# The last load of the experts' weights issued as 16 transfers of eight partitions in place of one of 128

## The chip, the cores and the metric

The kernel runs on one core of a Trainium2 chip. The metric is the time of one execution on the device in microseconds (us), as the median of several runs. All views of the profile come from one execution, and their times are counted from the start of its span.

## The reference, cut to what matters

Three blocks follow each other in float32. The second, a soft mixture of experts, is the one whose weights the change loads.

```python
# 1: attention packed through 32 slots per head (8 batches, 8 heads, 576 positions, 64 wide)
out = sm_attn(q, sm_attn(p, k, v), sm_attn(p, k, v))      # softmax attention, twice
x = out as rows: (4608, 512)

# 2: soft mixture of 8 experts, 4 slots each
logits = x @ phi                                          # (4608, 32)
slot_input = softmax(logits over rows).T @ x              # (32, 512)
for e in range(8):
    h = maximum(slot_input[e] @ w1[e], 0)                 # w1[e]: 512 x 1024
    slot_out[e] = h @ w2[e]                               # w2[e]: 1024 x 512
x = softmax(logits over slots) @ slot_out                 # (4608, 512)

# 3: dense layer with SoLU and layer norm
h = x @ w_in                                              # 512 -> 1024
solu = h * softmax(h)
y = (solu - mean) / sqrt(var + 1e-6) * g_ln
return y @ w_out                                          # (4608, 512)
```

Part 3 needs the outputs of all experts before its first row: each row of `x` is a mix over all 32 slots.

## The kernel before, in words

The kernel has three stages. Stage 1 is the attention, with the logits and the slot inputs summed on the way. Stage 2 sends the slot inputs through the experts and, at its end, multiplies the slot outputs into `w_in`: `sw` = `slot_out @ w_in`, which stage 3 uses in place of `w_in`. Stage 3 walks over 36 tiles of 128 rows: a product `h` with `sw` (L1416), softmax and norm statistics on DVE, ACT and POOL, two transposes, and the product `o` with `w_out` (L1592, L1598, the last tile also L1605).

All loads go out from SP, in one order fixed in the list `order`, into a ring of 14 slots of 128 x 2304 floats (four more slots join later): keys, queries, values, `w_in`, `w_out`, and then the experts' weights as 29 loads `("w", 0)` to `("w", 28)`. Those weights are cut into 256 granules of 128 x 256 floats, nine to a load. Load 27 goes out in three parts of one, four and four granules (`CUTS`), and load 28, the last, has the four granules that are left: 128 partitions of 4 KB. The function `load` (L308) issues them; the line of the experts' weights is L321.

The first four experts are computed one after the other (`mk_w1`, L1039, and `mk_w2`, L1090). The second products of the last four experts come as the last 64 granules, ordered by quarter `k` of the model width and by expert within it (`mk_block`, L1132). A block takes four granules, eight matmuls. The last two blocks are quarter 3 of experts 6 and 7: the first of them reads the last part of load 27, the second reads load 28 and nothing else reads that load. After the last block of a quarter ACT copies the sum out (L1143), PE turns it (L1147), ACT writes it to `SO`, and PE multiplies that into `sw` (L1350): quarters 0 to 2 as they come, quarter 3 at the end. Then ACT and DVE write `sw` out in two parts (L1358, L1362), and the first `h` of stage 3 follows.

The order of instructions on each engine is written out by a planner (`Plan`) before anything runs: it simulates the engines with the costs given to `op`, and the instructions are then emitted in that order. Every engine takes its instructions in that order at run time. A load stands in the plan as one step of the engine "DMA", with 317 ns a granule; the function that the step calls may issue several transfers. Semaphores are put in by the framework. A DMA from SP gets one of eight semaphores in turn, and SP does not issue it before the transfer that had the same semaphore eight issues earlier has landed.

Of the kernel before, what the change touches and what calls it, by code (L numbers as in the profile page):

```python
# [185 lines left out]
def pack_attention__soft_moe__solu_kernel(  # L186
# [13 lines left out]
    nc = tc.nc  # L200
# [20 lines left out]
    NSPLIT = 1  # L221
    CH = (0, 2, 4, 8)
    NMOVE = 4
    NRUN = 400
    NLATE = 500
    NTRY = 3500
# [26 lines left out]
    with ExitStack() as p12, tc.manual_schedule():  # L253
# [54 lines left out]
        def load(key, part):  # L308
            def go():
                if part == 0:  # L310
                    pool = W["ring2"] if key in RING2 else ring
                    loaded[key] = pool.tile([128, RW], FP32, tag="r", name="r")
                t = loaded[key]
                if key[0] in "kq":
                    c0, c1 = (1152 * c for c in halves(key)[part:part + 2])
                    nc.sync.dma_start(out=t[:, c0:c1], in_=(kT if key[0] == "k" else qT)[key[1]][:, c0:c1])
                elif key[0] == "v":
                    nc.sync.dma_start(out=t, in_=v[key[1], key[2]])
                elif key[0] == "w":
                    c0, c1 = (256 * c for c in cuts(key[1])[part:part + 2])  # L320
                    nc.sync.dma_start(out=t[:, c0:c1], in_=w12[key[1]][:, c0:c1])  # L321
                else:
                    src = (w_out if key[0] == "wo" else w_in)[key[1]].bitcast(UINT32)
                    nc.sync.dma_start(out=t[:, :2048].bitcast(UINT32), in_=src)

            return go

        def halves(key):
            return (0, 1, 2) if key[1] == 0 else (0, 2)

        def cuts(i):
            return CUTS.get(i, (0, min(9, 32 * NE - 9 * i)))
# [1043 lines left out]
        plan.goals = [(x, 1.0), (o_SIT, 0.3), (o_lo, 0.1)]  # L1376
        plan.trials = NRUN
        plan.then = [(NLATE, set(range(o_2, len(plan.ops))))]
# [7 lines left out]
    with ExitStack() as p3, tc.manual_schedule():  # L1386
# [329 lines left out]
        for k in range(NT):  # L1716
            mk_tile(k, ([*range(8), *range(32, 36), *range(8, 32)])[k])
            if k == NMOVE - 1:
                plan.moved = set(range(n0, len(plan.ops)))
# [63 lines left out]
```

## Time and profile before

| | us |
|---|---|
| median of 3 runs | 399.81 (398.6 to 400.46) |
| the profiled execution | 398.32 |
| its span in the profile | 396.5 |
| PE busy / DVE / ACT / POOL | 375.6 / 285.4 / 232.6 / 205.9 |
| stage 1 to about | 126 |
| stage 2 to about | 181 |

The profile gives, for each engine, the time in which it ran an instruction. A chain of waits is followed back from the last instruction of the kernel, at each step to what released it, so what stands in the chain is what set the end in this execution. "SPq" is SP's queue, on which DMAs are issued; "DMA" in the chain is a transfer from its issue to its landing. "PEld" is the load of a matmul's weights, which runs ahead of the matmul. [...] In the views of PE an fp32 matmul counts as two.

### The profile page before, as it was taken

To read this page: it belongs to the slowest core of one execution; us is meant where nothing else is said; L and a number is where in the kernel's file an instruction comes from. 1 tells how busy PE (TensorE), PEld (TensorE's weight loads), DVE (VectorE), ACT (ScalarE), POOL (GpSimd) and SP (SyncE) were. 2 spreads that over 40 slices of the span, in tenths; PEclk is the share of its full clock that TensorE was granted. 3 is DMA by queue.
4 is the path that set the end of the run, shared out by engine and by line. 5 is a ranking of instruction groups with operands and counts; after the bars stand their busy time and mean duration, and the time that the engine had idled before them with its cause. 6 is when DMAs were issued, how large, how long until landed. Compare 5 with 4: busy or idle time off the path is not lost.

```text
span 396.5 us, 9563 instructions
## 1 busy us (share of the span) xinstructions
PE 375.6 (95%) x3760; PEld 198.0 (50%) x3760; DVE 285.4 (72%) x563; ACT 232.6 (59%) x437; POOL 205.9 (52%) x314
## 2 busy tenths in 40 slices
PE   8888999988989999798999999999999999999996
PEld 3456566656535664553444444444444444444445
DVE  2168899997977889917997766776677667766721
ACT  1447787887644654116978665666566656665610
POOL 1032456263234556892769665556555655565540
PEclk9999999998999999999999999999999999999999
DMA  8999999999999999940367956685776766756761
GB/s 308 423 419 416 418 419 415 419 418 414 421 416 421 421 414 422 416 189 1 62 128 157 185 122 145 136 158 120 147 157 135 122 145 156 138 119 145 140 152 54
DMA packets 89420, 99.25 MB, mean 250 GB/s; under 512 B 75936, under 2 KB 76576, under 8 KB 82080
## 3 DMA queue, kind: packets, MB, share of 16 engines
q1 hardware_dynamic: 89088, 98.58, 77.1%
q8 instruction: 29, 0.48, 0.5%
q14 instruction: 15, 0.12, 0.1%
q10 hardware_dynamic: 288, 0.07, 0.1%
HBM read 70.85 MB, written 9.44 MB: 202 GB/s over the span
## 4 chain that ended last, share of the span: by engine, by line
PE 62%; DMA 17%; DVE 13%; ACT 3%; issue 1%; POOL 1%; SPq 1%; DVEq 0%; ACTq 0%; POOLq 0%
PE o L1592 30%; PE o L1598 15%; DMA r<-w 8%; DMA r<-kT 6%; PE h L1416 3%; DMA r<-qT 3%; PE w L1039 3%; DVE bsum L603 2%; DVE bmx L583 2%; PE sc L411 1%; PE o L1605 1%; DVE nm L1424 1%; DVE nb L431 1%; PE sw L1350 1%; ACT a L436 1%
## 5 line engine op out<-in xcount | busy, mean ns | idle before, releaser
L1592 PE MATMUL o<-whi,th 128*128 128x512 f16 x280 | 106.1, 379 | 0.6 <-DVE nm L1424 0.5
L1592 PE MATMUL o<-wlo,th 128*128 128x512 f16 x280 | 106.1, 379 | 0.0
L1565 POOL TENSOR_TENSOR lo<-x,hi 128x1024 f16<-128x1024 f32 (+1 forms) x37 | 77.2, 2089 | 53.0 <-issue 47.1
L1592 PEld LDWEIGHTS <-th 128*128 128x128 f16 x560 | 54.5, 98 | 66.6 <-DMA th<-hi 1.5
L1440 ACT ACTIVATE e<-h,nm 128x1024 f32<-128x1024 f32 (+1 forms) x37 | 40.3, 1090 | 50.5 <-DVE nm L1424 50.5
L1598 PE MATMUL o<-whi,tl 128*128 128x512 f16 x280 | 66.5, 380 | 0.0
L1424 DVE TENSOR_REDUCE nm<-h 128x1 f32<-128x1024 f32 (+1 forms) x37 | 43.9, 1193 | 28.2 <-PE h L1416 28.2
L1497 ACT ACTIVATE e<-s3t,nv 128x1024 f32<-128x1024 f32 x35 | 40.2, 1147 | 10.9 <-DVE nmean L1462 10.9
L1543 ACT ACTIVATE hi<-s3t,nr,rs 128x1024 f16<-128x1024 f32 x35 | 43.4, 1240 | 5.1 <-POOL nr L1526 5.0
L1450 DVE SCALAR_TENSOR_TENSOR s3t<-h,e 128x1024 f32<-128x1024 f32 (+1 forms) x36 | 43.5, 1207 | 1.8
L1620 DVE TENSOR_TENSOR ob<-o,winv 128x512 f32<-128x512 f32 x35 | 24.2, 691 | 25.3 <-PE o L1598 25.3
L1598 PEld LDWEIGHTS <-tl 128*128 128x128 f16 x280 | 25.0, 98 | 34.0 <-issue 7.7
L1535 DVE TENSOR_SCALAR x<-s3t,nmean,rs 128x1024 f32<-128x1024 f32 x35 | 30.7, 877 | 0.4 <-POOL rs L1522 0.4
L1416 PE MATMUL h<-swr,cT 96*128 96x512 f32 x72 | 28.8, 483 | 1.2 <-DVE swr L1362 0.9
L469 POOL TENSOR_SCALAR r<-s 128x1 f32<-128x1 f32 x16 | 4.4, 274 | 39.7 <-ACT a L436 39.6
L395 PE MATMUL w<-wz 128*128 128x512 f16 x83 | 22.9, 379 | 0.5 <-DVE A L590 0.4
L1522 POOL TENSOR_TENSOR rs<-rs,half 128x1 f32<-128x1 f32 x36 | 20.2, 560 | 2.8
L1039 PE MATMUL w<-r,SIT 128*32 128x256 f32 x256 | 21.5, 383 | 0.0
L436 ACT ACTIVATE a<-sc,nb 128x576 f32<-128x576 f32 x16 | 11.8, 739 | 13.8 <-DVE nb L431 13.5
L431 DVE TENSOR_REDUCE nb<-sc 128x1 f32<-128x576 f32 x16 | 11.6, 753 | 10.4 <-PE sc L411 10.2
L1416 PEld LDWEIGHTS h<-swr,cT 96*128 96x128 f32 x72 | 13.6, 190 | 7.6 <-issue 1.5
L1287 POOL TENSOR_TENSOR r<-ua,ux 128x512 f32<-128x512 f32 x8 | 10.6, 1335 | 12.6 <-DMA r<-w 4.5
(227 smaller groups left out, 644.6 us busy)
## 6 DMA issues: line engine op xcount, KB each, us to landing
r<-w SPq DMA_DIRECT2D x27, 1152.0 KB, 17.5
r<-v SPq DMA_DIRECT2D x8, 1152.0 KB, 21.1
r<-kT SPq DMA_DIRECT2D x7, 1152.0 KB, 22.1
r<-qT SPq DMA_DIRECT2D x7, 1152.0 KB, 22.0
out<-ob SPq DMA_DIRECT2D x31, 256.0 KB, 2.3
r<-w_in SPq DMA_DIRECT2D x4, 1024.0 KB, 21.9
r<-w_out SPq DMA_DIRECT2D x4, 1024.0 KB, 21.6
r<-w SPq DMA_DIRECT2D x3, 512.0 KB, 17.0
```

The lines of the kernel that those rows point to most:

```text
L1039: nc.tensor.matmul(out=hp[32 * g:32 * g + 32, 0:256], lhsT=SIT[:, k, :], rhs=gran(i), start=(k == 0), stop=(k == 3),)
L1416: nc.tensor.matmul(out=w, lhsT=cT[t % 4][:, t // 4, :], rhs=swr[n], start=True, stop=True)
L1424: nc.vector.tensor_reduce(out=z["nm"][:, h:h + 1], in_=hcols(h), axis=AX.X, op=ALU.max, negate=True)
L1440: nc.scalar.activation(out=z["e"][:, cols(h)], in_=hcols(h), func=ACTF.Exp, bias=z["nm2"] if h else z["nm"][:, 0:1], accum_out=z["S"][:, h ...
L1450: nc.vector.scalar_tensor_tensor(out=z["s"][:, cols(h)], in0=hcols(h), scalar=z["f"] if H == 2 and h == 0 else 1.0, in1=z["e"][:, cols(h)] ...
L1497: nc.scalar.activation(out=z["e"], in_=z["s"], func=ACTF.Square, bias=z["nv"], scale=2.0 ** -15, accum_out=z["V"])
L1535: nc.vector.tensor_scalar(out=z["x"][:, cols(h)], in0=z["s"][:, cols(h)], scalar1=z["n"], scalar2=z["r"], op0=ALU.add, op1=ALU.mult,)
L1543: nc.scalar.activation(out=z["hi"][:, cols(h)], in_=z["s"][:, cols(h)], func=ACTF.Identity, scale=z["r"], bias=z["nr"])
L1565: nc.gpsimd.tensor_tensor(out=z["lo"][:, cols(h)], in0=z["x"][:, cols(h)], in1=z["hi"][:, cols(h)], op=ALU.subtract)
L1592: nc.tensor.matmul(out=z["o"], lhsT=z["th"][:, c, :], rhs=w[:, c, :], start=(c == 0 and w is whi), stop=False)
L1598: nc.tensor.matmul(out=z["o"], lhsT=z["tl"][:, c, :], rhs=whi[:, c, :], start=False, stop=(c == 7))
L1620: nc.vector.tensor_tensor(out=z["ob"], in0=z["o"], in1=winv, op=ALU.mult)
```

## The change

The load of the experts' weights goes out in strips of `s` partitions. For load 28 `s` is 8, for all others it is 128, which is the loop's single pass. The planner's step of load 28 stays one step.

```diff
@@ -221,6 +221,7 @@
     NSPLIT = 1
     CH = (0, 2, 4, 8)
     NMOVE = 4
+    FEW = 8
     NRUN = 400
     NLATE = 500
     NTRY = 3500
@@ -318,7 +319,9 @@
                     nc.sync.dma_start(out=t, in_=v[key[1], key[2]])
                 elif key[0] == "w":
                     c0, c1 = (256 * c for c in cuts(key[1])[part:part + 2])
-                    nc.sync.dma_start(out=t[:, c0:c1], in_=w12[key[1]][:, c0:c1])
+                    s = FEW if key[1] == 28 else 128
+                    for r in range(0, 128, s):
+                        nc.sync.dma_start(out=t[r:r + s, c0:c1], in_=w12[key[1]][r:r + s, c0:c1])
                 else:
                     src = (w_out if key[0] == "wo" else w_in)[key[1]].bitcast(UINT32)
                     nc.sync.dma_start(out=t[:, :2048].bitcast(UINT32), in_=src)
```

## Rows read from the trace of the kernel before

**Rows 1.** The page, busy time and share of the span of PE.
```profile
PE 375.6 (95%) x3760; PEld 198.0 (50%) x3760; DVE 285.4 (72%) x563; ACT 232.6 (59%) x437; POOL 205.9 (52%) x314
```

**Rows 2.** Chain of waits from 155 to 192 us: start, duration, what.
```profile
157.81 16.96 DMA r<-w
...
174.81 0.65 PE w L1132 x16
...
176.48 0.57 PE w L1132 x16
...
178.51 1.97 PE sw L1350 x4
...
190.23 1.73 PE o L1592 x8
```

**Rows 3.** Stage 3: length, busy us of PE, PEld, DVE, ACT, POOL, PEclk, DMA share, GB/s.
```profile
190.60:387.90 197.30, 196.70 (x910) 91.71 (x908) 140.63 (x240) 124.61 (x174) 121.23 (x207) 1.00 0.68 139
```

**Rows 4.** Timeline of PE, 172 to 182 us: start, duration, instruction, idle before.
```profile
175.38 1.10 PE L1350 MATMUL sw<-wif,SO 128*96 128x512 f32 x2
...
176.41 0.64 PE L1132 MATMUL w<-r,hz 128*32 128x128 f32 x16
```

**Rows 5.** Line 321, windows with one issue each: start of the issue, time to landing.
```profile
L321 SPq DMA_DIRECT2D r<-w x1: 328/328/328, 145.2 to 145.2; - x1
...
L321 SPq DMA_DIRECT2D r<-w x1: 328/328/328, 157.8 to 157.8; - x1
...
DMA to landing us min/median/max: 17.0/17.0/17.0
...
L321 SPq DMA_DIRECT2D r<-w x1: 328/328/328, 160.7 to 160.7; - x1
...
DMA to landing us min/median/max: 15.4/15.4/15.4
```

**Rows 6.** What SP waited for, 148 to 162 us: total, times, longest.
```profile
SPq L321 <- DMA r<-w: 9.2, 4, 2.6
```

**Rows 7.** Timeline of SP, three stretches: DMA issues.
```profile
107.56 1.75 SPq L321 DMA_DIRECT2D r<-w  x4
...
2.58 0.64 SPq L336 DMA_DIRECT2D p_sb<-pT  x1
...
160.65 0.33 SPq L321 DMA_DIRECT2D r<-w  x1
```

**Rows 8.** DMA issues by line: KB each, median us from issue to landing.
```profile
out<-ob SPq DMA_DIRECT2D x16, 64.0 KB, 1.7
...
p_sb<-pT SPq DMA_DIRECT2D x1, 128.0 KB, 2.4
```

**Rows 9.** Busy time by stretches, around both falls of the clock and beside.
```profile
88.19:91.60 3.41, 1.97 (x28) 1.29 (x29) 3.20 (x13) 2.30 (x7) 1.90 (x5) 1.00 1.00 416
91.60:95.02 3.42, 3.42 (x29) 2.72 (x35) 3.39 (x8) 2.41 (x7) 1.36 (x2) 0.50 1.03 421
159.87:163.28 3.41, 1.86 (x44) 1.22 (x38) 3.26 (x6) 0.24 (x2) 1.64 (x2) 1.00 1.02 418
...
391.98:395.38 3.40, 1.25 (x12) 0.88 (x9) 0.42 (x1) 0.00 (x0) 0.00 (x0) 1.00 0.22 74
395.39:396.50 1.11, 0.00 (x0) 0.00 (x0) 0.00 (x0) 0.00 (x0) 0.00 (x0) 0.50 0.00 0
```

**Rows 10.** PE by groups, 91.7 to 95.0 us, then 40 to 91 us.
```profile
L651 PE MATMUL w<-ident,A 128*128 128x128 f32 x8 | 2.0, 401 | 0.2 <-POOL A L615 0.2
...
L651 PE MATMUL w<-ident,A 128*128 128x128 f32 x16 | 2.5, 283 | 0.2 <-POOL A L615 0.2
```

**Rows 11.** Busy time by stretches of one us, 170 to 176 us.
```profile
170.00:171.00 1.00, 1.00 (x14) 0.54 (x7) 0.00 (x0) 0.00 (x0) 1.00 (x3) 1.00 0.98 381
...
173.00:174.00 1.00, 0.99 (x36) 0.62 (x28) 0.00 (x0) 0.27 (x1) 1.00 (x1) 1.00 0.51 205
...
175.00:176.00 1.00, 1.00 (x18) 0.43 (x10) 0.00 (x0) 0.00 (x0) 1.00 (x2) 1.00 0.16 57
```

**Rows 12.** Tile cT, 143.3 to 146 us: strips of 32 partitions written.
```profile
L1181 POOL CAST cT<-chi x2: 1134/1193/1252, 143.6 to 144.8; 32x1152 fp32r<-32x1152 f32 x2
L1181 ACT CAST cT<-c_t x1: 1149/1149/1149, 143.5 to 143.5; 32x1152 fp32r<-32x1152 f32 x1
```

## The prediction

> **What bounds the kernel now.** I began with the page. PE is busy for 375.6 of 396.5 us [rows 1], but that is a mean over three stages, so I asked for the stretch of stage 3 alone: from 190.6 to 387.9 us PE is busy for 196.70 of 197.30 us [rows 3]. The reader is to see that stage 3 has no idle time left that could take in a later start: whatever its first `o` product loses, the end loses.
>
> Next I read the chain of waits up to that first `o` at 190.23 us [rows 2]. At the end of stage 2 it runs through the DMA queue: the third part of load 27 is issued at 157.81 us and is 16.96 us under way, so it lands at 174.77; PE runs the block that reads it at 174.81. Then come a piece of `sw`, the last block at 176.48 in the chain, `sw` of quarter 3 at 178.51, and so on to the first `o`. So PE's way from the last loads to the first `o` is one chain.
>
> Where load 28 stands in it is read from two views. In the timeline of PE the last block starts at 176.41, right behind a piece of `sw` that began at 175.38 and took 1.10 us [rows 4]. Load 28 is issued at 160.7 us and lands 15.4 us later, at 176.0 [rows 5]. So the transfer that the change cuts up lands some 0.4 us before PE comes to it: it is not waited for, but nearly. A gain of load 28 alone is worth nothing, and a loss over 0.4 us is on the path.
>
> The last thing to read is what SP does. It waits for landings of earlier weight loads four times between 148 and 162 us, 9.2 us in all [rows 6]. The issue of load 28 shows for what: the transfer issued eight before it, at 145.2 us, took the same 15.4 us and landed at 160.6 [rows 5], and load 28 goes out at 160.65 [rows 7]. At most eight transfers are out at a time, and their landings let SP go on.
>
> **The change part by part.** *What it removes.* One issue of 512 KB, 0.33 us of SP [rows 7], hidden behind transfers that have 15 us to go. Worth nothing.
>
> *What it adds.* Sixteen issues of 32 KB, and sixteen turns in the count of eight. Strips 1 to 8 take the semaphores of the eight transfers in flight, in the order in which these land. The eighth of these is the last part of load 27, so strip 8 can't go out before its landing at 157.8 + 17.0 = 174.8 us [rows 5]. Until then nothing is lost. SP is in order, so strips 9 to 16 stand behind strip 8: eight more issues, all after 174.8 us. Their own semaphores are those of strips 1 to 8; strip 1 was in the queue behind load 27's last part and lands about then, and the others follow, so I count no further wait for them, only the issues.
>
> One issue behind another costs 0.44 us: four weight loads in a row took 1.75 us with the last one's 0.43 us, so three steps in 1.32 us [rows 7]. Bounds: 0.33 us, an issue by itself, and 0.64 us, the slowest in the first microseconds [rows 7]; no row has a transfer of eight partitions. I take 0.44, since that row is the same line with the same kind of wait. Eight steps are 3.5 us: strip 16 goes out at 178.3 us.
>
> From issue to landing a transfer into an idle queue takes 1.7 us (64 KB, a store) to 2.4 us (128 KB, a load in the first microseconds) [rows 8]. I take 2.0, the middle, as a strip is smaller than either. Strip 16 lands at 180.4 us, against 176.0 of the whole load before. The last block needs all sixteen, so PE starts it at 180.4 and not at 176.41: 4.0 us late. Bounds by the same rows: 8 x 0.33 + 1.7 = 4.3 gives a start at 179.1 and 2.7 us; 8 x 0.64 + 2.4 = 7.5 gives 182.3 and 5.9 us.
>
> *Who stands behind the wait.* On PE the next piece of `sw`, the turning of quarter 3 and its `sw`; on ACT and DVE the two parts of `sw` and then tile 0. All are links of the chain [rows 2], and all were early otherwise. SP's next work, the transposes and stores of stage 3, hangs on tile 0 and moves with it. The extra waits of the last block (eight semaphores in place of one) run out while PE stands still; I count nothing.
>
> *The clock.* PE has no work from about 176.5 to 180.4 us. In the trace the granted clock falls twice: after a stretch with PE busy for 1.97 of 3.41 us, and at the end, in 395.39, after one with 1.25 us busy and then none [rows 9]. It did not fall after 1.86 of 3.41 us with the experts' matmuls [rows 9], so busy time alone does not tell, but a stretch with nearly nothing in it is emptier than all of these. I expect a fall to 0.50 as PE comes back. The one in mid-kernel stayed for 3.42 us [rows 9], and in it the transposes of L651 took 2.0 us for eight, 0.25 each, against 2.5 for sixteen, 0.156 each, at full clock [rows 10]: 1.6 times. PE's links fill most of the first 4 us after the restart. Work of 3.4 us at 1.6 times the duration does what 2.1 us did: 1.3 us lost. Bounds: 0 (no fall, or the fall is over in the pause) and 1.7 us (twice the duration).
>
> *The sum.* 4.0 + 1.3 = 5.3 us. On the profiled execution, 398.32 us, that is 403.6; it ran 1.5 us below the median of the runs, 399.81, on which the forecast stands: 405.1 us.
>
> **The rivals.** *B: the wait without the fall.* The pause may be cut by where it falls, or be shorter. Then 399.81 + 4.0 = 403.8 us.
>
> *C: the queue, not the issues; not slower.* Were strips held by no landing, all would be out by 160.65 + 16 x 0.44 = 167.7 us and only bytes would count. The DMA engines don't end together: their share falls from 0.98 at 170 us over 0.51 at 173 to 0.16 at 175 [rows 11], so some are dry five us before others. If a strip of eight partitions goes to eight of the sixteen engines, these get twice their 32 KB, one part's time more: the parts of 512 KB go through in 176.0 - 174.8 = 1.2 us. On engines that lead this ends before 176.0 and the time stays at 399.8; on those that lag it ends at 174.8 + 2 x 1.25 = 177.3, 0.9 us late: 400.7. It decides from the point where strips no longer wait for landings. SP's waits [rows 6] speak against that. [...]
>
> *D: each strip waits for the one before it,* because all write one tile. From 174.9 us on fifteen strips at 2.0 us: 30 us, so load 28 lands near 205 and the time is about 429 us. Against it: strips of 32 partitions of the same tiles `cT` were written by POOL and ACT side by side [rows 12].
>
> *E: dearer issues.* 0.64 us each and 2.4 us to land: 5.9 + 1.3, so 407.0 us.
>
> **How the numbers follow.** Forecast 0.52, B 0.25, C 0.10, E 0.08, D 0.05. The range takes in B with a shorter wait (399.81 + 2.7 = 402.5, less some spread of the runs) and E: 402.2 to 407.1; outside are C, D and tails. About 0.5%, 2 us, is what can be told from no change. C lies within it, with little of B's shortest waits: same 0.10. Only a run far below its fellows would be faster: 0.02. Slower 0.88.
>
> **What will show it.** In the profile after: SP has sixteen issues of 32 KB at L321, eight of them from about 174.8 us, 0.44 us apart, where there was one; the last lands near 180.4. PE's last L1132 stands after an idle time of about 4 us with a DMA as its releaser, and load 28 enters the chain. PEclk has a stretch of 0.50 near 180 to 184 us. From the first `o` on everything is later by the same time and nothing else has changed. The prediction is wrong if the last eight issues start well before 174.8 us (then C), if they are 2 us apart (D), or if the last block comes late but the end does not.

## The result, and the profile after

The changed kernel takes 403.9 us (median of 5 runs, 401.86 to 405.79), the kernel before 398.6 beside it. The ratio, taken over all runs and not from the two medians, is 1.0109 (1.0081 to 1.0138): slower, as forecast. A second measurement on another chip, told below, gave 1.0127 (1.0111 to 1.0143). The order of the instructions on PE, ACT, DVE and POOL is the same in both kernels; SP has sixteen issues where it had one. Lines from 319 on are three or fewer higher than before: L321 is now L324, L1132 is L1135, L1350 is L1353.

The page after: PE's busy time answers to [rows 1]. It hardly changed, while the span grew from 396.5 to 402.4 us, so what came in is waiting.

```profile
span 402.4 us, 9586 instructions
...
PE 375.2 (93%) x3760; PEld 196.9 (49%) x3760; DVE 287.6 (71%) x563; ACT 232.5 (58%) x437; POOL 204.5 (51%) x314
```

The chain of waits of the changed kernel, around the end of stage 2 (start, duration, what), which answers to [rows 2]:

```profile
157.98 17.41 DMA r<-w
...
175.41 0.27 SPq L324
...
175.72 0.30 SPq L324
...
177.75 0.29 SPq L324
...
178.09 2.04 DMA r<-w
180.12 0.30 issue
180.43 0.64 PE w L1135 x16
...
182.79 3.16 PE sw L1353 x4
...
185.98 0.59 ACT swr L1361
```

The reader is to see SP in the chain, where it never stood before. The last part of load 27 lands at 175.39; SP then issues strips 8 to 16, the last eight steps from 175.41 to 178.09, so 0.336 us each; the last strip takes 2.04 us, and PE needs 0.30 us more for its waits. By the trace its operand now stands behind eight semaphores in place of one.

PE's timeline in the changed kernel (start, duration, instruction, idle before and releaser), which answers to [rows 4]:

```profile
176.00 1.10 PE L1353 MATMUL sw<-wif,SO 128*96 128x512 f32 x2
180.43 0.64 PE L1135 MATMUL w<-r,hz 128*32 128x128 f32 x16 [3.32 <-DMA r<-w]
...
182.79 3.15 PE L1353 MATMUL sw<-wif,SO 128*96 128x512 f32 x4 [0.30 <-ACT SO L1077]
```

The last block begins at 180.43 and not at 176.41 [rows 4]: 4.02 us late. The last pair of `sw` takes 3.15 us where it took 1.97 [rows 2]. The stretches of the changed kernel (length, busy us of PE, PEld, DVE, ACT, POOL, the granted clock of TensorE as a share of full speed (PEclk), DMA share, GB/s) show why:

```profile
177.00:180.40 3.40, 0.10 (x1) 0.00 (x1) 0.00 (x0) 0.00 (x0) 1.12 (x1) 1.00 0.24 65
...
181.82:185.23 3.41, 3.11 (x6) 1.30 (x5) 0.00 (x0) 0.59 (x2) 0.00 (x0) 0.50 0.00 0
```

PE stood still for 3.3 us, and 1.4 us after it came back its clock was at 0.50 for 3.41 us. By the chains the last pair of `sw` ends at 185.95 instead of 180.48: 5.47 us late. Of these 4.02 were there when the block began, and 1.45 come behind it, with the clock at 0.50: 0.26 on the way from the block to that pair (2.36 us in place of 2.10) and 1.19 in the pair itself.

### The profile page after: what moved, and what is told of

It is laid out like the page before. It is cut to its first block, busy times and chain, and to the rows that moved or that the text cites. A ratio compares the mean times of both kernels' runs of the same rounds, so it can differ in the third digit from the quotient of the medians.

```text
span 402.4 us, 9586 instructions
## 1 busy us (share of the span) xinstructions
PE 375.2 (93%) x3760; PEld 196.9 (49%) x3760; DVE 287.6 (71%) x563; ACT 232.5 (58%) x437; POOL 204.5 (51%) x314
## 4 chain that ended last, share of the span: by engine, by line
PE 58%; DMA 19%; DVE 13%; ACT 5%; issue 2%; SPq 1%; POOL 1%; ACTq 0%; DVEq 0%; POOLq 0%
PE o L1595 28%; PE o L1601 14%; DMA r<-w 9%; DMA r<-kT 6%; PE h L1419 3%; DMA r<-qT 3%; PE w L1042 3%; DVE bsum L606 2%; DVE bmx L586 2%; PE o L1608 1%; PE sc L414 1%; PE sw L1353 1%; DVE bsum L610 1%; DVE nb L434 1%; DMA th<-hi 1%
## 5 line engine op out<-in xcount | busy, mean ns | idle before, releaser
L1453 DVE SCALAR_TENSOR_TENSOR s3t<-h,e 128x1024 f32<-128x1024 f32 (+1 forms) x36 | 43.4, 1207 | 2.0 <-issue 0.2
L1538 DVE TENSOR_SCALAR x<-s3t,nmean,rs 128x1024 f32<-128x1024 f32 x35 | 32.7, 935 | 0.4 <-POOL rs L1525 0.4
L497 PE MATMUL w<-r,aT 128*32 128x64 f32 (+1 forms) x640 | 14.8, 223 | 2.8 <-issue 2.1
```

The source lines that it names most:

```text
L1453: nc.vector.scalar_tensor_tensor(out=z["s"][:, cols(h)], in0=hcols(h), scalar=z["f"] if H == 2 and h == 0 else 1.0, in1=z["e"][:, cols(h)] ...
L1538: nc.vector.tensor_scalar(out=z["x"][:, cols(h)], in0=z["s"][:, cols(h)], scalar1=z["n"], scalar2=z["r"], op0=ALU.add, op1=ALU.mult,)
```

## The experiments

All runs stand beside the kernel before on the same chip; the edits are to the changed kernel.

**32 strips of 4 partitions: is it the issues behind the landing?**

```diff
-    FEW = 8
+    FEW = 4
```

> Load 28 in 32 transfers of 4 partitions. Theory: 24 issues after the landing of load 27's last part, 16 more than in the changed kernel at 0.34 us: the last block starts at about 185.8 us, 5.4 us later than in the changed kernel, and the time is 9 to 11 us above before. Rival (fewer engines): a quarter of the engines moves 128 KB each, four times 1.25 us after 174.8: the last block at about 179.8 us, no later than in the changed kernel.

Measured: 410.13 us, ratio 1.028 (1.0262 to 1.0298), 11.2 us more by the ratio. The end of the chain in this run:

```profile
183.19 1.85 DMA r<-w
185.04 0.33 issue
185.37 1.08 PE w L1135 x16
```

The last block starts at 185.37, 4.94 us after that of the changed kernel; 5.4 were forecast. SP's steps are 0.34 us again. The block is 10.3 us behind the landing of load 27's last part (175.09), where it was 5.0 behind with 16 strips: 5.2 us more, and sixteen further issues at 0.336 us make 5.4. The rival, a quarter of the engines, would have had the block at 179.8, no later than in the changed kernel: it falls. The time is a little above the 9 to 11 us that were forecast; the clock was at 0.50 for 10.24 us from 182.44 on, longer than in either profile of the changed kernel.

**8 strips of 16 partitions: do issues in front of the landing cost anything?**

```diff
-    FEW = 8
+    FEW = 16
```

> Load 28 in 8 transfers of 16 partitions. Theory: strips 1 to 7 go out while the big loads are still under way and cost nothing; only strip 8 is issued after the landing of load 27's last part, and lands 2.0 us later, so with 0.3 us of waits for eight semaphores PE's last block starts 2.4 us after that landing, at about 177.2 us, 0.8 us later than before; no fall of the clock; 0.8 to 1.5 us slower than before. Rival (each transfer costs the same wherever it stands): half of the changed kernel's loss, 2.2 to 2.7 us slower.

Measured: 400.14 us, ratio 1.0045 (1.003 to 1.006), 1.8 us more. By PE's timeline the block started at 178.26; the last part of load 27 was issued at 157.91 and landed after 17.96 us, at 175.87. So the block stood 2.4 us behind the landing, as forecast to the tenth. But that landing was itself 1.1 us later than before, which neither theory had, and so the 1.8 us lie outside both forecasts.

**16 transfers of all partitions: is it the strips' shape?**

```diff
-                    s = FEW if key[1] == 28 else 128
-                    for r in range(0, 128, s):
-                        nc.sync.dma_start(out=t[r:r + s, c0:c1], in_=w12[key[1]][r:r + s, c0:c1])
+                    s = 64 if key[1] == 28 else c1 - c0
+                    for c in range(c0, c1, s):
+                        nc.sync.dma_start(out=t[:, c:c + s], in_=w12[key[1]][:, c:c + s])
```

> Load 28 in 16 transfers again, but each of 128 partitions and 64 columns, so that every transfer uses all engines. Theory (eight transfers in flight at most, so eight issues and one landing come after the last part of load 27 has landed): as in the changed kernel, PE's last block starts 5 us after that landing (at about 180.4 us), with 0.34 to 0.44 us between issues; 4 to 6 us slower than before. Rival (strips of eight partitions use half the engines, and that is the loss): with all engines used the last block starts at about 177 us and the time is within 1 us of before.

Measured: 404.7 us, ratio 1.0156 (1.0123 to 1.0188), 6.2 us more. The chain, from the landing on:

```profile
176.15 0.02 issue
176.17 0.33 SPq L324
176.50 0.04 issue
176.54 0.43 SPq L324
...
179.86 3.53 DMA r<-w
183.39 0.14 issue
183.52 0.60 PE w L1135 x2
```

Sixteen issues over all 128 partitions cost as much, and a little more: an issue with 128 partitions takes 0.43 us and a step 0.47, near the 0.44 read from [rows 7], against 0.336 for a strip, and the last transfer, in rows of 256 bytes, lands after 3.53 us. So the block stands 7.4 us behind the landing of load 27's last part and not 5. In this run that part landed at 176.15; a lag of that size was there already when loads 23 and 25 landed (164.78 and 170.40, in the kernel before 163.63 and 169.07). The first packet of the small transfers ran at 169.4 by the trace, so the lag is not put down to the cut.

**Zeros in the pause: what does the clock cost?**

```diff
+                    if k == 3 and end:
+                        t = bank2()
+                        for _ in range(14):
+                            nc.tensor.matmul(out=t, lhsT=wz[:, 0:128], rhs=wz, start=True, stop=True)
                     if g0 == s0 and start:
```

> The changed kernel with 14 matmuls of zeros (3.0 us of PE) put in front of the last block, into the pause; they write a bank that nobody reads. Theory: the pause for the strips stays, the last block starts at about 180.4 us, but the clock does not fall behind it, the two last pieces of sw take 1.96 us and not 3.15, and the end comes 1.2 us earlier than in the changed kernel, 3 to 4.5 us above before. Rival (what the clock costs is hidden elsewhere): the same time as the changed kernel within 0.5 us.

Measured: 402.21 us, ratio 1.0094 (1.0078 to 1.011). PE's timeline in this run:

```profile
176.51 3.19 PE L1130 MATMUL v<-wz 128*128 128x512 f16 x14
179.83 0.64 PE L1139 MATMUL w<-r,hz 128*32 128x128 f32 x16
180.41 1.10 PE L1357 MATMUL sw<-wif,SO 128*96 128x512 f32 x2
181.93 1.96 PE L1357 MATMUL sw<-wif,SO 128*96 128x512 f32 x4 [0.30 <-ACT SO L1077]
```

The block waits as long (4.9 us behind the landing, which was at 174.95), but the pair of `sw` is back at 1.96 us and the clock stays at 1.00. By the ratios of two chips (1.0109 and 1.0094) the gain is only 0.6 us, with intervals that overlap. Since the changed kernel had been timed elsewhere, both were run again side by side.

> The changed kernel once more, to stand beside the next run on one chip. Theory: 4.2 to 5.5 us above before, a stretch of the clock at 0.50 behind the pause, the last block about 5 us after the landing of load 27's last part. Rival (the first measurement was high by chance): under 3 us.

> The changed kernel with 14 matmuls of zeros in the pause once more, beside the changed kernel on one chip. Theory: 1.0 to 1.5 us faster than the changed kernel, from the clock alone. Rival (the clock's cost is hidden): within 0.4 us of it.

Measured: 404.36 us for the changed kernel (1.0127, 1.0111 to 1.0143) and 402.04 with the zeros (1.0074, 1.0061 to 1.0087): 2.3 us apart, about twice the forecast of the clock's part; the changed kernel itself is 5.1 us above before by the ratio, as forecast. The profile of the changed kernel from this second measurement shows a reason, in one stretch:

```profile
179.41:186.24 6.83, 5.48 (x23) 2.68 (x24) 0.00 (x0) 0.63 (x3) 1.39 (x2) 0.50 0.01 2
```

and in PE's timeline:

```profile
180.46 1.08 PE L1135 MATMUL w<-r,hz 128*32 128x128 f32 x16 [3.25 <-DMA r<-w]
...
184.03 3.04 PE L1353 MATMUL sw<-wif,SO 128*96 128x512 f32 x4 [0.30 <-ACT SO L1077]
```

Here the clock was at 0.50 for 6.83 us, twice as long as in the first profile, and covered nearly all of PE's way from the block (180.46) to the end of the last pair of `sw` (187.07): 6.61 us, against 4.07 in [rows 2, 4] (176.41 to 180.48), so the clock cost 2.5 us in this execution. The clock can fall elsewhere too: with the zeros side by side it was at 0.50 for 6.83 us from 163.64 on, ahead of the pause. So the 2.3 us are a difference between executions with several such falls, and not the price of this one alone.

**The strips five loads earlier: does a full queue hide them?**

```diff
-                    s = FEW if key[1] == 28 else 128
+                    s = FEW if key[1] == 24 else 128
```

> The 16 strips of eight partitions for load 24 (9 KB a partition) in place of load 28, five loads ahead of the last, with 15 us of transfers queued in front. Theory: the eight in flight are then all small strips, so the queue runs dry wherever it is done: strips 9 to 16 and then load 25 are issued only after load 23 has landed at about 160.6 us, load 25 at about 163.3 in place of 147.4; everything behind is later by 2.5 to 4 us and the kernel is 2.5 to 5 us slower than before. Rival (only the end of the queue is exposed, transfers queued in front hide the issues): within 0.7 us of before.

Measured: 408.26 us, ratio 1.0235 (1.0206 to 1.0264), 9.4 us more. A full queue hides nothing: the rival falls. But the loss is twice the theory's. Three stretches of this run:

```profile
164.00:168.00 4.00, 2.84 (x38) 2.25 (x38) 4.00 (x5) 0.27 (x1) 4.00 (x4) 0.50 0.33 76
...
168.20:169.10 0.90, 0.75 (x1) 0.39 (x2) 0.90 (x1) 0.10 (x1) 0.90 (x2) 0.50 0.53 82
...
172.00:176.00 4.00, 0.00 (x0) 0.00 (x0) 0.00 (x0) 0.00 (x0) 4.00 (x5) 0.50 0.98 111
```

From 164 to 168 us the queue has run dry, as forecast: SP waits for the landing of load 23 until 165.13 and then for strips, and the share is 0.33. The theory had that landing at 160.6, which is load 22's; load 23 landed at 163.63 in the kernel before and at 165.12 here. From 168.20 to 169.10 only strips are in the queue (load 25 goes out at 169.18): the share is 0.53 and 82 GB/s are moved, where half of the 420 GB/s of full loads would be 210. A packet of 9 KB takes 0.94 us there by the trace, in full loads 0.35. So strips of eight partitions are slow in themselves, besides that eight of them at a time don't keep the queue filled; why, no run shows. From 172 to 176, with load 25 in the queue too, the engines are 98% busy and move 111 GB/s, and every packet takes about 1.3 us, those of the full load too. The clock was at 0.50 for 17.07 us from 163.93 on, which is part of the 9.4 us and was not in the theory.

**4 strips of 32 partitions: a control that failed.**

```diff
-    FEW = 8
+    FEW = 32
```

> Load 28 in 4 transfers of 32 partitions. Theory: all four go out before the last part of load 27 has landed (at 160.7 to 169.1 us), so nothing is issued behind that landing; PE's last block starts at the same distance from it as before, 1.6 us, and the time is within 1 us of before. Rival (every cut costs, in proportion to the number of transfers): a quarter of the changed kernel's loss, 1.1 to 1.3 us slower, and half of that of 8 transfers.

Measured: 401.43 us, ratio 1.0063 (1.0041 to 1.0085), 2.5 us more, half the changed kernel's loss, more than either side had forecast and no less than 8 strips cost. The issue is early in all four, so the theory, as it stood, is not the whole. By PE's timeline the block stood 1.65 us behind the landing of load 27's last part, as before; what moved was that landing. The issue of that part and its time to landing, which answer to [rows 5]:

```profile
L324 SPq DMA_DIRECT2D r<-w x1: 328/328/328, 158.2 to 158.2; - x1
...
DMA to landing us min/median/max: 18.8/18.8/18.8
```

It landed at 177.0 and not at 174.8, though it was issued ahead of every strip. Three runs were to tell why.

> Load 28 in 4 transfers of 128 partitions and 256 columns (1 KB a partition), beside the 4 strips of 32 partitions, which cost 2.5 us although all four went out early: there the last part of load 27 landed at 177.0 us, 2.2 us later than before. Theory A (strips of partitions hold up the engine that lags, as the leading ones then write the strips in front of its last big loads): with whole-height transfers load 27's last part lands at about 174.8 us again and the time is within 0.7 us of before. Theory B (any four transfers in place of one do it): again about 177 us and 2 to 3 us slower.

> Load 28 in 2 transfers of 64 partitions. Theory A: still strips, so load 27's last part lands late, between 175.5 and 177 us, and the kernel is 1 to 2.5 us slower, though nothing is issued late. Theory B (by number of transfers): half of the loss of four, 1.2 us. If neither, within 0.5 us of before: four strips are then more than twice as bad as two.

> The kernel before once more, for a second look at how far the landing of load 27's last part varies by itself. Theory A: 174.3 to 175.3 us, so the 177.0 of the strips of 32 is not chance. Rival (it varies by 2 us from one execution to the next): anywhere from 174 to 177, and times that spread as widely as those of the strips, 3 us; the runs of before so far spread by 1.1 us.

The first has 256 in place of 64 columns in the edit by columns above, the second `FEW = 64`. Measured: four transfers by columns 398.57 us, ratio 1.0014 (0.9997 to 1.0031), no loss, and load 27's last part landed at 157.8 + 17.0 = 174.8; two strips of 64 partitions 401.38 us, 1.0072 (1.0053 to 1.0091), 2.9 us more, somewhat above theory A's range, with that landing at 177.2; the kernel before against itself 1.0016 (0.9999 to 1.0034), and its last part landed at 157.9 + 17.0 = 174.9 again. Two cuts by partitions cost more than four by columns: theory A holds in kind, B falls.

One forecast of the rival came true: the twelve runs of the kernel before spread over 3.0 us (398.21 to 401.2). Its four slowest runs are those with the lowest granted clock, 0.987 to 0.991. Its profile is of one of these and shows a cause that is not the landing: the clock was at 0.50 for 6.83 us while PE worked through the experts, and the last block began at 178.47 in place of 176.41.

```profile
163.43:170.26 6.83, 6.47 (x72) 4.16 (x74) 5.47 (x5) 0.48 (x2) 6.83 (x7) 0.50 1.00 411
```

The profile with two strips has no such fall before its end (granted clock 1.000).

Not all of the late landing belongs to the strips. Load 25, which landed before any part of the first strip, was already 0.3 us late with strips of 32 partitions and 0.7 with strips of 64. From its landing to that of load 27's last part it took 5.7 us in the kernel before (5.8 in its second profile) and 5.7 with four transfers by columns; 7.4 with strips of 64 partitions, 7.6 with 32, 6.8 with 16, and 6.1 and 5.9 in the two profiles with strips of eight. So strips of 64 and 32 cost that part 1.7 and 1.9 us, and strips of eight at most 0.2 to 0.4, little more than the 0.1 between the two profiles of the kernel before. With strips of 64 the second strip itself then landed only at 179.37, and PE's last block waited for it, not for load 27. What the strips do is seen in the stretch from 170 to 172 us, when the last loads overlap: in the kernel before the first of sixteen updates of load 28's semaphore came at 171.0, and the last of load 26's at 171.9. First the kernel before:

```profile
170.00:172.00 2.00, 2.00 (x16) 0.70 (x8) 0.00 (x0) 0.00 (x0) 2.00 (x4) 1.00 0.82 315
```

Two strips of 64 partitions:

```profile
170.00:172.00 2.00, 2.00 (x38) 1.28 (x33) 0.42 (x1) 0.00 (x0) 2.00 (x4) 1.00 1.03 244
```

Four transfers by columns:

```profile
170.00:172.00 2.00, 2.00 (x20) 0.75 (x8) 0.55 (x1) 0.00 (x0) 2.00 (x4) 1.00 0.93 337
```

With strips the engines are busier (1.03 against 0.82) and move less (244 against 315 GB/s): the transfers stand in each other's way. By columns 0.93 moves 337. The packets in the trace tell it apart: those of 9 KB, which belong to load 26 and earlier, take 0.35 us in this stretch in the kernel before and with columns, and 0.58 to 0.62 with strips of 64 or 32 partitions. So the strips slow down transfers that were issued long before them. My reading, from these packets and from the spread of the updates, is that the engines that lead are already at the strip while those that lag still write the loads before it, and that the two hinder each other. Where they would meet is not shown; no run here tells the side that is written from the side that is read.

## Why the prediction was right, step by step

*SP's issues behind the landing, 3.5 us.* Right in kind; the size was 2.7: a step of 0.336 us and not 0.44. The row that I took was of transfers with 128 partitions; such steps are 0.47 us in the run by columns, strips are cheaper.

*The landing of the last strip, 2.0 us.* 2.04.

*"Until then nothing is lost."* Wrong: load 27's last part landed at 175.39 in place of 174.77, 0.6 us late, of which 0.2 were there when load 25 landed. Strips of 64 and 32 partitions held that part up by 1.7 and 1.9 us. I had read the queues as first come, first served on each engine, and overlooked that the parts of one load land up to five us apart (in the kernel before the sixteen updates of load 28's semaphore came from 171.0 to 176.0); that what the leading engines write holds up the others is my reading of the 1.7 and 1.9 us.

*"I count nothing" for the waits.* Wrong by 0.30 us on PE behind the landing. In stage 3, where tiles take over the ring's memory, ACT and DVE wait for the strips' semaphores too. These rows are from the changed kernel's chain:

```profile
205.66 0.04 ACTq L1546
...
205.89 0.04 ACTq L1546
205.93 0.20 issue
206.13 0.19 ACT e L1500
```

The four waits take from 205.66 to 205.93, and nobody has to be waited for any more: the strips landed 25 us earlier. Four such on DVE (L1453) stand in the chain at 191.4 to 191.8. From the end of the last pair of `sw` to the end of the span the changed kernel needs 216.5 us, before it was 216.1. That these waits are the 0.4 is not shown: the two profiles of the kernel before differ by as much, and the kernel with the zeros, which has the same waits, needs 215.9.

*The clock, 1.3 us.* Right in kind; 1.45 in this profile and 2.5 in the other one, where the fall lasted twice as long; 2.3 between the medians with and without the zeros.

The sum was 4.0 + 1.3 = 5.3. Measured in the profile: 4.02 to the last block (0.62 from the landing, 2.68 + 2.04 + 0.30 from issues, last strip and waits, less 1.6 of distance that PE had before), 1.45 of the clock, 0.4 in stage 3: 5.9, the growth of the span. That the 4.0 us to the last block came out so exactly is luck: an issue that was priced too high paid for the landing and the waits, which were left out. By the ratios the kernel lost 4.3 us in the first measurement and 5.1 in the second; the forecast of 405.1 also stood on a time before of 399.81, where 398.6 was measured beside the changed kernel.

Of the rivals, B (no fall of the clock) has nearly the measured median, 403.8, but only from that higher time before; it falls by the clock at 0.50 in both profiles. E falls by the step of 0.336 us, C (the bytes on half the engines) falls by the run with columns, D by the first strip landing beside the second, 0.2 us apart. That a strip goes to eight of sixteen engines and doubles their bytes, the term of C's sum, no run shows; the trace has eight updates of a strip's semaphore as data landed (and one just behind the issue), where the whole load 28 had sixteen. At the end of the stream the bytes did not set the pace: the share was 0.35 from 177 to 178 us and 0.38 from 178 to 179, below the 0.53 that strips reached five loads earlier.

## What to carry to other kernels

Where only a fixed number of transfers may be in flight (eight here), what counted was how many issues still had to come when the last big transfer landed. A cut by columns that had none left to come was free (four transfers: 1.0014, within the noise). Beyond that each cost an issue, 0.34 to 0.47 us, and one landing of 2 to 3.5 us came on top. In the middle of the stream the sixteen strips cost more, 9.4 us, as the transfers behind waited too. A cut by partitions was not free even when it went out early: two strips of 64 lost 2.9 us. And a new pause on TensorE can cost more than its length: with 3.3 us without work the clock was at 0.50 in both profiles of the changed kernel, for 3.41 and 6.83 us.

## What the runs showed of the hardware

- Transfers into eight partitions, alone in the queue: 82 GB/s at a share of 0.53, 0.94 us for a packet of 9 KB, against about 420 GB/s and 0.35 us of full loads. With a full load beside them: 111 GB/s at a share of 0.98.
- Transfers into 64 or 32 partitions delayed a transfer issued before them, the last part of load 27, by 1.7 and 1.9 us, with packets of 9 KB at about 0.6 us in place of 0.35. Four transfers of all partitions did not: 5.7 us from load 25's landing to that part's, as before.
- An issue from SP takes 0.29 us for strips of four or eight partitions and 0.43 us for 128 partitions, when they follow one another; from one to the next it is 0.336 and 0.47 us.
- The fall of the clock behind a pause of 3.3 us lasted 3.41 us in one execution of the same kernel and 6.83 us in another. The kernel before had a fall of 6.83 us in one execution, from 163.43 on, and none there in another.
